# Scores of two heads side by side in float32 from head 18 on, and a mixing addition at high priority

## The chip, the cores and the metric

The kernel runs on one core of a Trainium2 chip. A core has TensorE (PE; PEld is its loading of weights) for matmuls, VectorE (DVE) and ScalarE (ACT) for work on elements, GpSimd (POOL) for the same beside them, and SyncE (SP), which issues the DMAs here. Each engine takes its instructions in order and waits at semaphores for the others. The metric is the time of one execution on the device in microseconds, the median of several runs.

## The reference

Attention over blocks of 64 tokens, a mixing of tokens and channels, and a gate, in float32. There are 8 sequences of 8 heads, 576 tokens and 64 elements a head; the channels are 512.

```
scores = scale * q @ k.T                    # 64 heads of 576 x 576, depth 64
scores = where(block_i >= block_j, scores, -1e9)
attn = softmax(scores);  x = attn @ v       # heads side by side: 8 x 576 x 512
h = (x.T @ U) @ V;  u = x + h.T             # mixing of tokens, rank 32
x = u + max(u @ w_ch1, 0) @ w_ch2           # mixing of channels, 2048 wide
gate = sigmoid(causal convolution of x, 5 taps)
out = (gate * (x @ w_val)) @ w_out
```

## The kernel before

The heads are walked in order. The kernel writes the order of TensorE's instructions itself; those of the other engines are put in order by a scheduler, from the order of the program and from priorities. A generator `attention` steps through the heads in ticks. The tick of head n computes its scores, its maximum and its exponentials, and, two heads behind, the products of the weights with v (`emit_pv`). Between them stand the steps of the mixing of tokens for the pairs before: T (transposes), G (product with U) and H (product with V, then the addition to x).

After the heads of the first sequence the channel mixing runs too, over nine groups of 512 tokens. Each of its steps s is a block of twelve matmuls of 512 columns into h (`emit_h1`, L841) and twelve into acc (`emit_o`, L887). In the midst of each block and behind it, `gap` takes steps of the generator, as a pace set by counts allows. So a tick is spread over several blocks, and a `yield` in it is a place where a block of six matmuls can stand.

Most matmuls are done in float32r: an operand is split into a high part, which float32r keeps, and the rest as a second float32r number, and three matmuls add the products. A matmul in float32 itself shows as two records of weights and matmul in the trace, one in float32r as one.

The 64 heads have two forms. Heads 0 to 17 (`n < NQ`) compute scores with rows and columns exchanged (`emit_q_bank`), in float32. From head 18 on, which the change is about, before has `prep_qk` and `emit_s_piece`:

- `prep_t` transposes q and k of a pair of heads on VectorE into `tq` and `tk`. Head a of the pair owns rows 64a to 64a + 63.
- `prep_qk` makes of them for one head operands of 128 rows: `qs` has the high part of q on the head's own rows and the rest on the other 64, `ks` the high part of k on both halves, and `kl` the rest of k on its own rows and zeros on the others. This takes three casts on ScalarE (L93) and a memset (L380) and two subtractions (L99) on GpSimd.
- `emit_s_piece` makes the scores of one head in four groups, with a yield behind each. The groups have query columns of 64, 192 and 256 (one PSUM buffer), 320, 448 and 320. Each piece takes two matmuls, `ks` with `qs` (L397) and `kl` with `qs` (L398). ScalarE copies the group to SBUF (L402).

PSUM buffers for scores (pS), products with v (pPV) and the mixing steps (pT, pG, pH) come from one ring of four (L204, `ABUF`). The SBUF tiles for scores, `s0` and `s1`, have two buffers each. Behind the scores come memsets at the masked corners on GpSimd (`emit_corners`), the maximum over keys on VectorE (`emit_max_a`, `_b`, `_c`), the subtraction (L528) and the exponentials (L550).

The keys of heads 0 to 17 lie padded with zeros in four tiles, whose room `ks` and `qs` take over. `mix_H` adds the product with V to x (L713) and by that also frees the PSUM buffer pH; x goes on to `u`, the operand of the channel mixing. `behind(0)` in it does nothing, since no instruction is noted under 0.

Of the kernel before, what the change touches and what calls it, by code (L numbers as in the profile page):

```python
# [8 lines left out]
F32 = mybir.dt.float32  # L9
F32R = mybir.dt.float32r  # L10
# [7 lines left out]
P = 128  # L18
# [4 lines left out]
def attn_moe_gate_kernel(ctx: ExitStack, tc: tile.TileContext, q, k, v, U, V, w1, w2, wval, convw, wout, out):  # L23
    nc = tc.nc
    B, H, S, D = q.shape
# [8 lines left out]
    NP = H // 2  # L34
# [21 lines left out]
    ABUF = 4  # L56
    RAWB = 2
    WAB = 2
    QV = 10
    KV = 0  # L60
    UVE = 0
    HPOS = 8
    GPOS = 6
# [1 line left out]
    PRE = 2  # L65
    CV0 = 1
    CV1 = 3
    MX0 = 0
    TP0 = 0
    NR0 = 0  # L70
    MM0 = 0
# [3 lines left out]
    NQ = FIRST_SPLIT  # L75
# [11 lines left out]
    def f32(ap):  # L87
        return ap if ap.dtype == F32 else ap.bitcast(F32)

    vec, act, pool, pe, sp = nc.vector, nc.scalar, nc.gpsimd, nc.tensor, nc.sync  # L90

    def hi_act(o, i):
        act.copy(o, i)  # L93
# [4 lines left out]
    def lo(eng, o, i, h):  # L98
        eng.tensor_tensor(o, i, f32(h), op=ALU.subtract)  # L99
# [13 lines left out]
    def behind(at):  # L113

        return tc.issue_after(mark[at]) if at in mark else nullcontext()
# [83 lines left out]
    st_p = rpool("stp", 1)  # L199
    s_p = rpool("sp", 2)  # L200
# [85 lines left out]
    sw = []  # L286
# [17 lines left out]
    def setup_att():  # L304
        for t in vstk:
            pool.memset(t[:, :, D:P], 1.0)
            pool.memset(t[0:D, NK - 1, :], 0.0)
        for a in range(2):
            for t in kz:
                pool.memset(t[a][own[1 - a]], 0.0)  # L310

    raw = {}

# [23 lines left out]
    stk = {}  # L337

    own = [slice(0, D), slice(D, P)]
    def pads(nm, dtype):  # L340
        return [st_p.tile([P, S], dtype, tag=f"{nm}{a}", name=f"{nm}{a}") for a in range(2)]

    kz = [pads(nm, F32) for nm in ("ks", "qs")]
    ks, qs = [], []
    kl = st_p.tile([P, S], F32R, name="kl")
    qkt = {}

    def prep_t(pn):
        if pn >= B * NP:
            return  # L350
        t = raw.pop(pn)
        if 2 * pn < NQ:
            tq = rot("tk" if pn % 2 else "tq", 1)
            z = kz[pn % 2]
            for rows in own if pn == 0 else (slice(0, P),):
                vec.transpose(tq[rows], t["q"][rows])
                for a in range(2):
                    if pn or rows == own[a]:
                        vec.transpose(z[a][own[a]], t["k"][own[a]])
            qkt[pn] = (tq, z)  # L360
        else:
            tq, tk = rot("tq", 1), rot("tk", 1)
            vec.transpose(tq, t["q"])
            vec.transpose(tk, t["k"])
            qkt[pn] = (tq, tk)
        load_qk(pn + 1)

    def prep_qk(n):
        if n >= B * H or n < NQ:
            return  # L370
        if not ks:
            ks.extend(pads("ks", F32R))
            qs.extend(pads("qs", F32R))
        tq, tk = qkt[n // 2]
        a = n % 2
        me, ot = own[a], own[1 - a]
        hi_act(qs[a][me], tq[me])
        hi_act(ks[a][me], tk[me])
        hi_act(ks[a][ot], tk[me])
        pool.memset(f32(kl[ot]), 0.0)  # L380
        lo(vec if n < KV else pool, kl[me], tk[me], ks[a][me])
        lo(vec if n < QV else pool, qs[a][ot], tq[me], qs[a][me])

    def kslice(j):
        return slice(q0[j], q0[j] + P) if q0[j] + P <= S else slice(S - P, S)

    stt = {}

    def emit_s_piece(n, i):
        pr, a = divmod(n, 2)  # L390
        if i == 0:
            stt[n] = [s_p.tile([P, w], F32, tag=f"s{h}", name=f"s{h}") for h, w in enumerate(sw)]
        ps = psum["a"].tile([P, 512], F32, tag="a", name="pS")
        o = 0
        for j, a0, a1 in pieces[i]:
            w = a1 - a0
            pe.matmul(ps[:, o:o + w], ks[a][:, kslice(j)], qs[a][:, a0:a1], start=True, stop=False)  # L397
            pe.matmul(ps[:, o:o + w], kl[:, kslice(j)], qs[a][:, a0:a1], start=False, stop=True)  # L398
            o += w
        j, a0, a1 = pieces[i][0]  # L400
        d = soff[j] + a0 - q0[j]
        act.copy(stt[n][half_of[j]][:, d:d + o], ps[:, 0:o])  # L402


    qbanks = [
# [14 lines left out]
    def emit_q_bank(n, i):  # L420

        a = n % 2
        tq, z = qkt[n // 2]
        if i == 0:
            s0, s1 = (s_p.tile([P, w], F32, tag=f"s{h}", name=f"s{h}") for h, w in enumerate(sw))
            eqs[n] = {3: s0[:, 0:4 * P], 1: s0[:, 4 * P:6 * P], 0: s1[:, 0:P], 2: s1[:, P:4 * P], 4: rot("m" if a else "mb", 1)}
            t = tiny_p.tile([P, 2 * NTT + 2], F32, tag="rq", name="rq")
            qmax[n] = (t[:, 0:NTT + 1], t[:, NTT + 1:], psum["a"].tile([P, 512], F32, tag="a", name="pS"))
        r, nm, _ = qmax[n]
        ps = psum["a"].tile([P, 512], F32, tag="a", name="pS") if i else _  # L430
        for t, k0, k1, o in qbanks[i]:
            pe.matmul(ps[:, o:o + k1 - k0], tq[:, kslice(t)], z[a][:, k0:k1], start=True, stop=True)
        if i == 0:
            vec.memset(ps[0:D, 4 * P - D:4 * P], MASKED)
        elif i == 2:
            vec.memset(ps[0:D, 3 * P - D:3 * P], MASKED)
        elif i == 3:
            vec.memset(ps.rearrange("p (c w) -> p c w", w=D)[0:D, 1:6:4, :], MASKED)
        for t, k0, k1, o in qbanks[i]:
            c = t + (k0 > 0)  # L440
            vec.reduce_max(r[:, c:c + 1], ps[:, o:o + k1 - k0], axis=AX.X)
        if i == 0:
            x = vec.tensor_scalar(nm[:, 3:4], r[:, 3:4], -scale, None, op0=ALU.mult)
        elif i == 2:
            vec.tensor_tensor(r[:, 4:5], r[:, 4:5], r[:, 5:6], op=ALU.max)
            x = vec.tensor_scalar(nm[:, 2:5:2], r[:, 2:5:2], -scale, None, op0=ALU.mult)
        elif i == 3:
            x = vec.tensor_scalar(nm[:, 0:2], r[:, 0:2], -scale, None, op0=ALU.mult)
        if i == 1:
            eqs[n]["wait"] = ps  # L450
            return
        noted(1, x)
        noted(3, x)
        for t, k0, k1, o in qbanks[i] + (qbanks[1] if i == 2 else []):
            src = eqs[n]["wait"] if i == 2 and t == NTT - 1 and k0 == 0 else ps
            act.activation(eqs[n][t][:, k0:k1], src[:, o:o + k1 - k0], AF.Exp, bias=nm[:, t:t + 1], scale=scale)
# [241 lines left out]
    def mix_H(pn, i):  # L698
        pcs = mix_pieces(pn // NP)
        if i >= len(pcs):  # L700
            return
        gi, a0, a1, off = pcs[i]
        if gi >= 2 and gi > y_done[0] + 2:
            later.append((pn, i))
            return
        xt = xts[pn]
        d = pn % NP
        uh, ul = u_tiles(gi)
        w = a1 - a0
        ps = ps_p.tile([P, 512], F32, tag="a", name="pH")  # L710
        pe.matmul(ps[:, 0:w], gst[pn], vst[:, a0:a1], start=True, stop=True)
        with behind(MX0 if pn < NP else 0):
            vec.tensor_tensor(xt[:, a0:a1], ps[:, 0:w], xt[:, a0:a1], op=ALU.add)  # L713
        hi_act(uh[:, d, off:off + w], xt[:, a0:a1])
        lo(pool, ul[:, d, off:off + w], xt[:, a0:a1], uh[:, d, off:off + w])
# [7 lines left out]
    def tick(n, mixed, last=B * NP):  # L723


        e = n - DEPTH
        new, old = n < NH, 0 <= e < NH

        load_v(e + 1)
        for i in range(4):  # L730
            if n < NQ:
                emit_q_bank(n, i)
            elif new:
                emit_s_piece(n, i)
            if i == 3 and new and n >= NQ:
                emit_corners(n)
                emit_max_a(n)
            yield
        if new:
            if n >= NQ:  # L740
                emit_max_b(n)
            if n % 2 == 1:
                prep_t((n + 1) // 2)
            prep_qk(n + 1)
        yield from mixing(2 * e, mixed, last)
        if new and n >= NQ:
            for _ in emit_max_c(n):
                pass
            emit_sub(n, 0)
            emit_sub(n, 1)  # L750
        if old:
            emit_pv(e, 0)
            yield
        if new and n >= NQ:
            emit_exp(n)
        if old:
            emit_pv(e, 1)
        prep_v(e + 1)
        emit_est(e + 1)
        if old:  # L760
            if e % 2 == 1:
                with tc.high_priority() if URG and e == H - 1 else ExitStack():
                    emit_norm_a(e // 2)
                    emit_norm_b(e // 2)
            yield
        yield from mixing(2 * e + 1, mixed, last)
# [247 lines left out]
        split_w2(f)  # L1014
    setup_att()
    prep_t(0)
    prep_qk(0)
    pb1 = ExitStack()
    pbp = {}

# [151 lines left out]
```

## Time and profile before

| what | value |
|---|---|
| time, median of 3 runs | 1533.32 us (1531.53 to 1535.98) |
| the profiled execution | 1538.09 us, its span 1536.3 us |
| PE busy | 1427.0 us, 93% of the span, 6664 instructions |
| DVE busy | 1146.3 us, 75% |
| ACT busy | 789.5 us, 51% |
| POOL busy | 516.1 us, 34% |
| granted TensorE clock, mean | 0.976 |

Busy is the time in which an engine has an instruction in flight. Matmuls overlap: one of 512 columns has a record of about 0.40 us, and the next one starts 0.23 us after it. A clock of 1 is 2.4 GHz, and 0.5 is 1.2 GHz. The time has a little more than the span, which goes from the first instruction to the last. The idle time of an engine is put down to the instruction whose end released it.

### The profile page before, as it was taken

Reading aid. Unit: us, or ns where it says so; the run is one execution under the profiler, and the core shown is the slowest. Engines: PE = TensorE matmul, PEld = TensorE weight load, DVE = VectorE, ACT = ScalarE, POOL = GpSimd, SP = SyncE. Lnnn points to the kernel's source line nnn. Section 1 sums busy time; section 2 is a strip of 40 time slices with the busy share of each in tenths; the row PEclk is TensorE's granted clock in tenths of the full one; section 3 lists DMA queues with packets and bytes.
Section 4 is the critical chain, followed back from the end, with each engine's and each line's share of the span. In section 5 each row is a group of like instructions: output and inputs, shape, how many; then the busy total and the mean of one; then the engine's idle time right before and its main releaser. Section 6 shows DMA issues by size and latency. Waiting matters only on the chain. (4 is left out here: it accounts for less than half of the span.)

```text
span 1536.3 us, 20391 instructions
## 1 busy us (share of the span) xinstructions
PE 1427.0 (93%) x6664; PEld 1151.1 (75%) x6664; DVE 1146.3 (75%) x2252; ACT 789.5 (51%) x1639; POOL 516.1 (34%) x587
## 2 busy tenths in 40 slices
PE   5897899979989998999899989989999999999999
PEld 2665677868767787777687778768888888778887
DVE  7887874659887888788888878887624427399991
ACT  4785565546565665666476556655512212243432
POOL 3133232333435333534443444335104210353410
PEclk8998999989999999999999999999999999999999
DMA  7555662224233333333323333232225543323221
GB/s 171 142 133 167 204 194 79 79 80 103 79 81 114 85 86 105 92 79 89 109 79 90 92 92 93 78 85 90 77 83 198 174 135 123 105 68 103 78 74 69
DMA packets 246291, 163.58 MB, mean 106 GB/s; under 512 B 197669, under 2 KB 212261, under 8 KB 246186
## 3 DMA queue, kind: packets, MB, share of 16 engines
q1 hardware_dynamic: 246186, 162.29, 36.6%
q8 instruction: 53, 0.87, 0.2%
q14 instruction: 52, 0.43, 0.1%
HBM read 134.98 MB, written 27.26 MB: 106 GB/s over the span
## 5 line engine op out<-in xcount | busy, mean ns | idle before, releaser
L887 PE MATMUL acc<-hh,w 128*128 128x512 f32 x1152 | 408.4, 405 | 10.2 <-ACT hh L869 10.2
L887 PEld LDWEIGHTS acc<-hh,w 128*128 128x128 f32 x1152 | 220.7, 192 | 57.7 <-ACT hh L869 12.8
L841 PE MATMUL h<-uh,w1hi 128*128 128x512 f32 x576 | 239.1, 415 | 9.9 <-DVE hl L870 6.3
L887 PE MATMUL acc<-hl,w 128*128 128x512 f32 x576 | 230.2, 400 | 5.9 <-DVE hl L870 5.9
L841 PE MATMUL h<-uh,w1lo 128*128 128x512 f32 x576 | 228.2, 396 | 0.0
L841 PE MATMUL h<-ul,w1hi 128*128 128x512 f32 x576 | 228.0, 396 | 0.0
L870 DVE SCALAR_TENSOR_TENSOR hl<-h,hh 128x512 fp32r<-128x512 f32 x144 | 98.2, 682 | 116.1 <-ACT hh L869 115.4
L869 ACT ACTIVATE hh<-h 128x512 fp32r<-128x512 f32 x144 | 85.8, 596 | 154.3 <-PE h L841 147.4
L550 ACT ACTIVATE s<-s 128x448 f32<-128x448 f32 x92 | 65.5, 712 | 150.0 <-DVE s L528 149.0
L841 PEld LDWEIGHTS h<-uh,w1hi 128*128 128x128 f32 x576 | 110.7, 192 | 35.8 <-DVE hl L870 8.2
L402 ACT COPY s<-pS 128x320 f32<-128x320 f32 (+2 forms) x184 | 89.8, 490 | 80.9 <-PE pS L398 77.2
L887 PEld LDWEIGHTS acc<-hl,w 128*128 128x128 f32 x576 | 110.5, 192 | 27.5 <-DVE hl L870 8.2
L841 PEld LDWEIGHTS h<-uh,w1lo 128*128 128x128 f32 x576 | 109.7, 190 | 24.8
L841 PEld LDWEIGHTS h<-ul,w1hi 128*128 128x128 f32 x576 | 110.7, 192 | 18.3 <-issue 1.4
L528 DVE TENSOR_TENSOR s<-s,mb 128x64 f32<-128x64 f32 (+4 forms) x230 | 123.0, 598 | 1.3
L962 DVE SCALAR_TENSOR_TENSOR gt<-yb,cw,gt 128x516 f32<-128x516 f32 (+1 forms) x144 | 116.5, 839 | 1.4
L99 POOL TENSOR_TENSOR vlo<-vstk,vhi 128x320 fp32r<-128x320 f32 x46 | 54.3, 1180 | 161.1 <-ACT vhi L93 148.1
L99 POOL TENSOR_TENSOR yl<-yb,yh 128x512 fp32r<-128x512 f32 (+7 forms) x64 | 67.7, 1091 | 96.9 <-ACT yh L93 96.8
L99 POOL TENSOR_TENSOR ul<-xt,uh 128x512 fp32r<-128x512 f32 (+7 forms) x64 | 53.2, 840 | 132.6 <-ACT uh L93 131.9
L397 PE MATMUL pS<-qs,ks 128*128 128x320 f32 (+4 forms) x276 | 80.4, 309 | 6.3 <-ACT lt L614 4.2
L398 PE MATMUL pS<-qs,kl 128*128 128x320 f32 (+4 forms) x276 | 82.4, 302 | 0.0
L99 DVE TENSOR_TENSOR el<-s,eh 128x448 fp32r<-128x448 f32 x92 | 76.7, 859 | 5.2 <-issue 4.6
(152 smaller groups left out, 3105.5 us busy)
## 6 DMA issues: line engine op xcount, KB each, us to landing
w<-w_s SPq DMA_DIRECT2D x144, 512.0 KB, 3.2
rawq<-in_q_dram SPq DMA_DIRECT2D x128, 72.0 KB, 2.4
rawk<-in_k_dram SPq DMA_DIRECT2D x128, 72.0 KB, 2.5
out_dram<-ot SPq DMA_DIRECT2D x35, 256.0 KB, 2.0
raw<-in_moe_w_ch_dram SPq DMA_DIRECT2D x64, 128.0 KB, 2.3
raw<-in_moe_w_ch_dram SPq DMA_DIRECT2D x16, 512.0 KB, 4.2
vstk<-in_v_dram SPq DMA_DIRECT2D x64, 128.0 KB, 2.6
w_s<-wo SPq DMA_DIRECT2D x16, 512.0 KB, 3.6
```

Of the source, the lines that this page charges most:

```text
L99: eng.tensor_tensor(o, i, f32(h), op=ALU.subtract)
L397: pe.matmul(ps[:, o:o + w], ks[a][:, kslice(j)], qs[a][:, a0:a1], start=True, stop=False)
L398: pe.matmul(ps[:, o:o + w], kl[:, kslice(j)], qs[a][:, a0:a1], start=False, stop=True)
L402: act.copy(stt[n][half_of[j]][:, d:d + o], ps[:, 0:o])
L528: noted(3, vec.tensor_tensor(sv(n, j), sv(n, j), mb[:, q0[j]:], op=ALU.subtract))
L550: act.activation(s, s, AF.Exp, scale=scale)
L841: pe.matmul(ps[:, 0:n], w[:, d, fs], x[:, d, 0:n], start=(d == 0 and i == 0), stop=(d == ND - 1 and i == 2))
L869: act.activation(hh[:, 0:n], ps[:, 0:n], AF.Relu)
L870: latest[0] = vec.scalar_tensor_tensor(hl[:, 0:n], ps[:, 0:n], 0.0, f32(hh[:, 0:n]), op0=ALU.max, op1=ALU.subtract)
L887: pe.matmul(acc[d][:, 0:n], w[:, wi, ds], x[:, 0:n], start=(f == 0 and i == 0), stop=(f == NF - 1 and i == 2))
L962: vec.scalar_tensor_tensor(gt[d][:, 0:gw], y[:, d, j:j + gw], cw[:, d, j:j + 1], gt[d][:, 0:gw], op0=ALU.mult, op1=ALU.add)
```

## The change

For pairs 9 to 31 (heads 18 to 63) `prep_qk` and all its operands are gone. `emit_s_piece` now works on a pair, in the tick of its even head: for each piece one float32 matmul for either head, straight from `tk` and `tq`, with rows 0 to 63 for the even head and 64 to 127 for the odd one, into a PSUM buffer for each. In the odd tick the four yields stay, without scores. The corners and the first part of the maximum come behind the fourth group for the even head as before, and for the odd head at the first step of its own tick.

As the scores of two heads are now made at once, a third pair of score tiles is needed: heads with n % 3 == 1 take the tiles `za` and `zb`, which held the padded keys of the first heads, now as one tile for both heads of a pair. The addition in `mix_H` is traced at high priority, so the scheduler puts it ahead of other work that is ready.

```diff
-    QV = 10
-    KV = 0
...
-    MX0 = 0
...
-                pool.memset(t[a][own[1 - a]], 0.0)
+                pool.memset(t[own[1 - a], a, :], 0.0)
...
-    def pads(nm, dtype):
-        return [st_p.tile([P, S], dtype, tag=f"{nm}{a}", name=f"{nm}{a}") for a in range(2)]
-
-    kz = [pads(nm, F32) for nm in ("ks", "qs")]
-    ks, qs = [], []
-    kl = st_p.tile([P, S], F32R, name="kl")
+    def spare(nm, n):
+        return st_p.tile([P, n], F32, tag=nm, name=nm)
+
+    kz = [spare(nm, 2 * S).rearrange("p (a s) -> p a s", s=S) for nm in ("za", "zb")]
...
-    def prep_qk(n):
...
-        tq, tk = qkt[n // 2]
-        a = n % 2
-        me, ot = own[a], own[1 - a]
-        hi_act(qs[a][me], tq[me])
-        hi_act(ks[a][me], tk[me])
-        hi_act(ks[a][ot], tk[me])
-        pool.memset(f32(kl[ot]), 0.0)
-        lo(vec if n < KV else pool, kl[me], tk[me], ks[a][me])
-        lo(vec if n < QV else pool, qs[a][ot], tq[me], qs[a][me])
-
...
-    def emit_s_piece(n, i):
-        pr, a = divmod(n, 2)
+    def emit_s_piece(pn, i):
+
+        heads = (2 * pn, 2 * pn + 1)
+        tq, tk = qkt[pn]
         if i == 0:
-            stt[n] = [s_p.tile([P, w], F32, tag=f"s{h}", name=f"s{h}") for h, w in enumerate(sw)]
-        ps = psum["a"].tile([P, 512], F32, tag="a", name="pS")
+            for n in heads:
+                stt[n] = [spare(("za", "zb")[h], w) if n % 3 == 1 else s_p.tile([P, w], F32, tag=f"s{h}", name=f"s{h}") for h, w in enumerate(sw)]
+        ps = [psum["a"].tile([P, 512], F32, tag="a", name="pS") for _ in own]
         o = 0
         for j, a0, a1 in pieces[i]:
             w = a1 - a0
-            pe.matmul(ps[:, o:o + w], ks[a][:, kslice(j)], qs[a][:, a0:a1], start=True, stop=False)
-            pe.matmul(ps[:, o:o + w], kl[:, kslice(j)], qs[a][:, a0:a1], start=False, stop=True)
+            for t, me in zip(ps, own):
+                pe.matmul(t[:, o:o + w], tk[me, kslice(j)], tq[me, a0:a1], start=True, stop=True)
             o += w
         j, a0, a1 = pieces[i][0]
         d = soff[j] + a0 - q0[j]
-        act.copy(stt[n][half_of[j]][:, d:d + o], ps[:, 0:o])
+        for n, t in zip(heads, ps):
+            act.copy(stt[n][half_of[j]][:, d:d + o], t[:, 0:o])
...
-        with behind(MX0 if pn < NP else 0):
+        with tc.high_priority():
             vec.tensor_tensor(xt[:, a0:a1], ps[:, 0:w], xt[:, a0:a1], op=ALU.add)
...
-            elif new:
-                emit_s_piece(n, i)
-            if i == 3 and new and n >= NQ:
+            elif new and n % 2 == 0:
+                emit_s_piece(n // 2, i)
+            if i == (0 if n % 2 else 3) and new and n >= NQ:
                 emit_corners(n)
                 emit_max_a(n)
...
-            prep_qk(n + 1)
```

In the changed kernel lines move up by 17 to 19: the score matmul is L380, its copy L385, the addition of the mixing L696, hh and hl L851 and L852.

On TensorE, the first group of scores of a head before, between two blocks of h (names are output<-moving operand, weights; the shape is that of the weights' columns and the moving columns):

```order
L841 MATMUL h_2682<-uh,w1lo 128x512
L841 MATMUL h_2682<-uh,w1hi 128x512
L841 MATMUL h_2682<-ul,w1hi 128x512
L841 MATMUL h_2682<-uh,w1lo 128x512
L397 MATMUL pS<-qs_2603,ks_2601 128x64
L398 MATMUL pS<-qs_2603,kl 128x64
L397 MATMUL pS<-qs_2603,ks_2601 128x192
L398 MATMUL pS<-qs_2603,kl 128x192
L397 MATMUL pS<-qs_2603,ks_2601 128x256
L398 MATMUL pS<-qs_2603,kl 128x256
L841 MATMUL h_2682<-uh,w1hi 128x512
```

The same place now; x2 are the matmuls of the two heads:

```order
L823 MATMUL h_2669<-uh,w1lo 128x512
L823 MATMUL h_2669<-uh,w1hi 128x512
L823 MATMUL h_2669<-ul,w1hi 128x512
L823 MATMUL h_2669<-uh,w1lo 128x512
L380 MATMUL pS<-tq,tk 128x64 x2
L380 MATMUL pS<-tq,tk 128x192 x2
L380 MATMUL pS<-tq,tk 128x256 x2
L823 MATMUL h_2669<-uh,w1hi 128x512
```

Six matmuls of 128 rows for one head have become six of 64 rows for two heads; the blocks around them are the same, and at the odd head's tick nothing stands between them.

On ScalarE, one head's copies of scores (L402) before, among the exponentials of the head before (L550) and the casts (L93) of q and k for the next one:

```order
L93 CAST x<-pT 64x128
L402 COPY s_5083<-pS 128x512
L550 ACTIVATE s_4906<-s_4906 128x448
L869 ACTIVATE hh<-h_5074 128x512
L402 COPY s_5083<-pS 128x320
L550 ACTIVATE s_4907<-s_4907 128x768
L402 COPY s_5084<-pS 128x448
L93 CAST ks_2602<-tk 64x576 x2
L402 COPY s_5084<-pS 128x320
L93 CAST qs_2604<-tq 64x576
```

Now, in the tick of an even head (s_ and za, zb are the score tiles of its two heads):

```order
L851 ACTIVATE hh<-h_6713 128x512
L385 COPY s_6769<-pS 128x512
L385 COPY za<-pS 128x512
L385 COPY s_6769<-pS 128x320
L385 COPY za<-pS 128x320
L385 COPY s_6770<-pS 128x448
L385 COPY zb<-pS 128x448
L385 COPY s_6770<-pS 128x320
L385 COPY zb<-pS 128x320
L851 ACTIVATE hh<-h_6809 128x512
L90 CAST uh<-xt 128x256
```

The casts are gone, and the eight copies of a pair stand together between two relus of h.

On VectorE, the addition of the mixing before (L713), the transpose of the next k, and the maximum of one head (m, t, r):

```order
L713 TENSOR_TENSOR xt<-pH,xt 128x320
L364 STREAM_TRANSPOSE tk<-rawk 128x576
L870 SCALAR_TENSOR_TENSOR hl<-h_5636,hh 128x512
L490 TENSOR_TENSOR m<-s_5604,s_5605 128x448
L492 TENSOR_TENSOR m<-m,s_5605 128x320
L492 TENSOR_TENSOR m<-m,s_5604 128x192
L492 TENSOR_TENSOR m<-m,s_5604 128x64
L500 STREAM_TRANSPOSE t<-m 128x448
L502 TENSOR_REDUCE r_5668<-t 128x18
L99 TENSOR_TENSOR el<-s_5432,eh 128x448
L99 TENSOR_TENSOR el<-s_5433,eh 128x768
```

Now (L696 is the addition, L852 the rest of h; za and zb hold the scores of one head, s_ those of the other):

```order
L358 STREAM_TRANSPOSE tq<-rawq 128x576
L359 STREAM_TRANSPOSE tk<-rawk 128x576
L473 TENSOR_TENSOR m<-za,zb 128x448
L696 TENSOR_TENSOR xt<-pH,xt 128x320
L852 SCALAR_TENSOR_TENSOR hl<-h_5439,hh 128x512
L475 TENSOR_TENSOR m<-m,zb 128x320
L475 TENSOR_TENSOR m<-m,za 128x192
L475 TENSOR_TENSOR m<-m,za 128x64
L483 STREAM_TRANSPOSE t<-m 128x448
L485 TENSOR_REDUCE r_5473<-t 128x18
L473 TENSOR_TENSOR m<-s_5401,s_5402 128x448
```

The addition now stands right behind the first step of a maximum, the transposes of q and k stand ahead of it together, and the maxima of the pair's two heads run into each other.

## Rows read from the trace of the kernel before

**Rows 1.** Stage of heads 18 to 63: start:end, length, busy us of each engine (instructions), PEclk, DMA.

```profile
262.00:1100.00 838.00, 778.70 (x3784) 644.30 (x3783) 696.66 (x1362) 497.73 (x1015) 338.96 (x413) 0.97 0.33 90
```

**Rows 2.** Groups of TensorE, 262 to 1100 us: busy, mean ns | idle before, releasers.

```profile
L887 PE MATMUL acc<-hh,w 128*128 128x512 f32 x744 | 267.5, 406 | 10.2 <-ACT hh L869 10.2
...
L841 PE MATMUL h<-uh,w1hi 128*128 128x512 f32 x373 | 154.5, 414 | 6.7 <-DVE hl L870 3.2 <-ACT lt L614 2.3 <-ACT s L402 0.6
...
L887 PE MATMUL acc<-hl,w 128*128 128x512 f32 x372 | 149.8, 403 | 5.9 <-DVE hl L870 5.9
...
L397 PE MATMUL pS<-qs,ks 128*128 128x320 f32 (+4 forms) x276 | 80.4, 309 | 6.3 <-ACT lt L614 4.2 <-DVE x L99 1.9
...
L612 PE MATMUL pPV<-eh,vhi 128*128 128x448 f32 x132 | 49.4, 374 | 11.5 <-DVE hl L870 11.5
...
L672 PE MATMUL pT<-ident,xt 128*128 128x128 f32 x92 | 14.3, 279 | 6.4 <-DVE xt L713 6.4
...
L680 PE MATMUL pT<-ident,xt 128*64 128x128 f32 x23 | 6.5, 284 | 8.4 <-DVE xt L713 8.4
```

**Rows 3.** TensorE's timeline around the scores of one head: start, length in us.

```profile
588.57 0.19 PE L397 MATMUL pS<-qs,ks 128*128 128x64 f32 x1
...
588.71 0.34 PE L397 MATMUL pS<-qs,ks 128*128 128x192 f32 x1
...
589.25 0.39 PE L841 MATMUL h<-uh,w1hi 128*128 128x512 f32 x1
...
590.64 0.31 PE L397 MATMUL pS<-qs,ks 128*128 128x320 f32 x1
...
590.94 0.39 PE L887 MATMUL acc<-hh,w 128*128 128x512 f32 x1
...
592.32 0.37 PE L397 MATMUL pS<-qs,ks 128*128 128x448 f32 x1
...
592.73 0.40 PE L887 MATMUL acc<-hh,w 128*128 128x512 f32 x1
...
594.10 0.31 PE L397 MATMUL pS<-qs,ks 128*128 128x320 f32 x1
...
594.40 0.39 PE L841 MATMUL h<-uh,w1hi 128*128 128x512 f32 x1
```

**Rows 4.** TensorE's timeline around two float32 matmuls of an earlier head.

```profile
229.78 1.88 PE L432 MATMUL pS<-ks,tq 128*128 128x512 f32 x4
...
231.73 0.40 PE L841 MATMUL h<-ul,w1hi 128*128 128x512 f32 x1
231.96 0.40 PE L841 MATMUL h<-uh,w1lo 128*128 128x512 f32 x1
```

**Rows 5.** Groups of ScalarE, 262 to 1100 us.

```profile
L402 ACT COPY s<-pS 128x320 f32<-128x320 f32 (+2 forms) x184 | 89.8, 490 | 80.9 <-PE pS L398 77.2 <-DVE r L518 1.9 <-DVE el L99 1.4
...
L93 ACT CAST ks<-tk 64x576 fp32r<-64x576 f32 x88 | 59.0, 671 | 8.4 <-PE pS L397 6.0 <-DVE tk L364 1.4
...
L93 ACT CAST qs<-tq 64x576 fp32r<-64x576 f32 x44 | 29.5, 671 | 0.5
```

**Rows 6.** Groups of GpSimd, 262 to 1100 us.

```profile
L99 POOL TENSOR_TENSOR qs<-tq,qs 64x576 fp32r<-64x576 f32 x45 | 69.0, 1533 | 8.3 <-ACT qs L93 5.7
...
L99 POOL TENSOR_TENSOR kl<-tk,ks 64x576 fp32r<-64x576 f32 x45 | 64.4, 1431 | 3.1
...
L380 POOL MEMSET kl<- 64x576 f32 x45 | 25.9, 575 | 74.4 <-PE pS L398 65.8 <-DVE hl L870 4.0 <-DVE t L499 4.0
```

**Rows 7.** The copy of 32x18 (min/median/max in the second row), and one collision.

```profile
L516 DVE COPY r<-r 32x18 f32<-32x18 f32 x46 | 41.2, 896 | 1.5
...
L516 DVE COPY r<-r x46: 166/168/1904, 285.3 to 1093.6; 32x18 f32<-32x18 f32 x46
...
738.63 1.41 POOL L99 TENSOR_TENSOR kl<-tk,ks 64x576 fp32r<-64x576 f32 x1
...
739.33 0.88 DVE L518 COPY r<-r 64x18 f32<-64x18 f32 x1
```

More of the change, by code (lines that the diff above doesn't have):

```diff
@@ L358, in prep_t @@
                     if pn or rows == own[a]:
-                        vec.transpose(z[a][own[a]], t["k"][own[a]])
+                        vec.transpose(z[own[a], a, :], t["k"][own[a]])
             qkt[pn] = (tq, z)
@@ L366, in prep_t @@
         load_qk(pn + 1)
-    def prep_qk(n):
[L369 to L373, printed above, removed]
-        tq, tk = qkt[n // 2]
-        a = n % 2
-        me, ot = own[a], own[1 - a]
-        hi_act(qs[a][me], tq[me])
-        hi_act(ks[a][me], tk[me])
-        hi_act(ks[a][ot], tk[me])
-        pool.memset(f32(kl[ot]), 0.0)
-        lo(vec if n < KV else pool, kl[me], tk[me], ks[a][me])
-        lo(vec if n < QV else pool, qs[a][ot], tq[me], qs[a][me])
     def kslice(j):
@@ L431, in emit_q_bank @@
         for t, k0, k1, o in qbanks[i]:
-            pe.matmul(ps[:, o:o + k1 - k0], tq[:, kslice(t)], z[a][:, k0:k1], start=True, stop=True)
+            pe.matmul(ps[:, o:o + k1 - k0], tq[:, kslice(t)], z[:, a, k0:k1], start=True, stop=True)
         if i == 0:
@@ L1016, in attn_moe_gate_kernel @@
     prep_t(0)
-    prep_qk(0)
     pb1 = ExitStack()
```

## The prediction

> **What bounds the kernel now.** I read three views in this order: the busy time by stage, then the idle time of TensorE inside the stage that changes, then single stretches of its timeline. The scores of heads 18 to 63 run from about 262 to 1100 us, woven between the blocks of the channel mixer (h, acc). In these 838 us TensorE has a record in flight for 778.7, VectorE for 696.7, ScalarE for 497.7 and GpSimd for 339.0 [rows 1]. So TensorE is nearly full, and a change can move the time in two ways only: by the array time of the scores, or by the 59.3 us in which TensorE stands idle, to which comes the granted clock of 0.97 there, worth at most 838 x 0.03 = 25 us (the clock has the levels 1.2 and 2.4 GHz, and 0.97 is their mix). Of the 59.3 us, seven groups hold 55.4, and each was released by VectorE or ScalarE: by hl 11.5 + 5.9 us, by hh 10.2, by the mixing addition xt (L713) 6.4 + 8.4, and 6.7 before h and 6.3 before pS behind hl and behind copies that empty PSUM [rows 2]. No wait of the scores for data stands among them. These are delays of two loaded queues, VectorE at 83% and ScalarE at 59%, and not one long chain.
>
> **The scores on TensorE.** Before, one head takes 12 float32r matmuls in four groups. From the start of a group to the start of the matmul behind it: 588.57 to 589.25 (0.68 us), 590.64 to 590.94 (0.30), 592.32 to 592.73 (0.41), 594.10 to 594.40 (0.30) [rows 3]. That is 1.69 us a head and 3.38 a pair; 23 pairs make 78 us.
>
> After, a pair has 12 float32 matmuls on 64 rows each, six for either head. The price of a float32 matmul is in the first heads' scores: two of 512 columns, four records, begin at 229.78. The block behind them has its second matmul at 231.73, and one of its matmuls takes 231.96 - 231.73 = 0.23, so the scores ended at about 231.50 [rows 4]: 0.43 us a record, two records a matmul, 0.84 ns a column and pass. By that a pass is 0.27 us at 320 columns, 0.38 at 448, 0.22 at 256, 0.16 at 192; at 64 I take 0.07, since two records of 64 fit between 588.57 and 588.71 [rows 3]. No row of before has a matmul on 64 rows, so how far the two heads overlap is bounded from both sides. Not at all: four passes after each other, 4 x (0.07 + 0.16 + 0.22 + 0.27 + 0.38 + 0.27) = 5.48 us a pair, +2.1, and 23 pairs make +48. Fully: two passes, 2.74 us, -0.64, in all -15. I take what lies between. In the queue stand A's first pass, A's second, B's first, B's second. A's second pass needs the same rows as A's first; B's first can run beside A's second; B's second then runs alone. A group that stands alone costs three passes: 0.81 + 1.14 + 0.81 for the single pieces. Within the first group of three pieces the halves interlock, about 0.07 + 0.07 + 0.16 + 0.16 + 0.22 + 0.22 + 0.22 = 1.12. That is 3.88 a pair, +0.50, and **+12 us** over 23 pairs. In the order of the changed kernel nearly every group does stand alone between two blocks: 90 groups for 23 x 4.
>
> At each of these groups the array goes from 128 rows to 64 and back. Rows of before show matmuls of one kind following each other 0.23 us apart while each has 0.40 us from start to end [rows 4]: 0.17 us of every matmul lie under the next one. If a change of rows let nothing overlap, 2 x 90 changes would cost up to 180 x 0.17 = 31 us; the lower end is nothing, since a change can't make the matmul before it shorter. I take nothing, the nearest row being the 128x128 transposes, float32r and float32 matmuls that already follow each other here without a gap of their own, and keep 31 for the rivals.
> By the Trainium skill, "TensorEngine Tiling (Array Packing)", Key Properties, changing the tiling mode, not just the tile, drains the engine. No row here shows such a change of mode, so the trace neither agrees nor differs; by that rule the sum would be 31 us worse than mine, and it is a rival below.
>
> **What goes from the other engines.** ScalarE loses two casts of k and one of q a head: 59.0 + 29.5 = 88.5 us of the stage's 497.7 [rows 5]. GpSimd loses two subtractions and a memset: 69.0 + 64.4 + 25.9 = 159 of 339 [rows 6]. VectorE loses no instruction, but time: a copy of 32x18 has a median of 168 ns and a mean of 896 [rows 7], so 46 x 0.73 = 33 us of it are spent standing still. The copy of 64x18 at 739.33 took 0.88 us while kl's subtraction ran on GpSimd from 738.63 to 740.04 [rows 7]. Not all such delays are due to the subtractions that go; xt's scaling and y's addition stay. By the share of GpSimd's time that goes I count about half, some 20 to 30 us of 697.
>
> None of that is on TensorE's queue, so it counts only as far as the waits of [rows 2] shrink. The addition of the mixing at high priority aims at 6.4 + 8.4 = 14.8 us; it also waits in VectorE's queue for its matmul pH, so I take 10 and not all. Of the other 40.6 us I take 12: VectorE's load falls from 83% to about 80%, ScalarE's from 59 to 49%, and waits behind a queue fall faster than its load. With 22 of 59.3 us of idle time gone, the same share of the 25 us of clock, 9, comes back. Together **-31 us**; the bounds are 0 and the 55.4 us of the named waits with their part of the clock, 79. What hides: nothing queued on GpSimd or ScalarE becomes late by the removal; next in line are the same waits for hl and hh.
>
> **What is added elsewhere.** The eight copies of scores (0.49 us each, [rows 5]) of a pair now stand together in the even head's tick, in ScalarE's queue ahead of hh and the exponentials, and none in the odd one; their number stays 184. The transposes of q and k now feed the matmuls directly, from single buffers, but the score matmuls that read them stand half a pair's work ahead of the next transposes, so I count nothing. The third pair of score tiles takes the place of the padded keys; est of the head three before has read it by then. Both maximum chains of a pair fall together on VectorE; that is within the bounds of the relief.
>
> **Sum.** The profiled execution had 1538.1 us (span 1536.3, the rest lies around it); 1538.1 + 12 - 31 = 1519. The median of the runs is 4.8 lower, 1533.3, so on that scale **1514 us**.
>
> **The rivals.**
> Full overlap: the two heads' first passes also start together, -15 instead of +12. For it: a group's operands lie on separate rows, in separate PSUM tiles. Against: each matmul is two records in the queue, and the queue has shown only one matmul after the other. 1533.3 - 15 - 31 = 1487 us.
> By the Trainium skill, "TensorE: Matmul & The Clock Gate", Part 3, matmuls on different row groups start about 4 ns apart and run together; no run here shows it, and by that the sum would be nearest to this case.
> No side by side at all: the float32 matmuls of 64 rows run one after the other, and the change does not do what its words say. The place is the four groups of a pair, the price +48; it decides from the point at which less than a third of the passes overlap, since the relief is 31. For it: all matmuls in the trace of before follow one another. 1533.3 + 48 - 31 = 1550 us, slower.
> Changing the rows costs: overlap as forecast, but each change of rows exposes up to 0.17 us, +31. For it: the tail under the next matmul is there in [rows 4]. Against: no present change of kind exposes it. 1533.3 + 12 + 31 - 31 = 1545 us, slower.
> PSUM in the place of casts: a group takes two of the four PSUM buffers that scores, PV, transposes, G and H share, and the next group waits for two copies. If every second of the 90 groups waits for one copy more, 45 x 0.49 = 22 us. For it: pS already waits 6.3 us for buffers [rows 2], and the copies stand together. Against: a block of six matmuls, about 1.4 us, stands between groups, and two copies take 1.0. 1533.3 + 12 + 22 - 31 = 1536 us, no change.
>
> **How the numbers follow.** Forecast 0.47, full overlap 0.12, no overlap 0.17, changes of rows 0.13, PSUM 0.11. The forecast's own range is 1500 to 1527 (relief of 18 to 45 us). What a measurement can tell from no change is 0.3%, 4.6 us, so 1528.7 to 1537.9 is the same. Faster: 0.47 + 0.12 = 0.59. Same: the PSUM case, 0.11. Slower: 0.17 + 0.13 = 0.30. The range from 1487 to 1556 takes in the centres of all cases; outside are a relief near zero with no overlap, and more relief than 31 with full overlap, together about 0.15 to 0.2.
>
> **What would show it.** On TensorE a pair's group of 320 columns should span about 0.8 us to the next block: 1.1 would be no overlap, 0.55 full, 1.0 and more with a late start of the next block the changes of rows. ScalarE's busy time should fall by about 90 us, GpSimd's by about 160, the 32x18 copy's mean below 600 ns. The waits for xt should be near 5 us and TensorE's idle time between 262 and 1100 us near 37. If the idle time is not below 50, the relief is wrong; if the groups stand at 1.1 us, the overlap is, and the kernel is slower.

## The result and the profile after

| | before | after |
|---|---|---|
| median of the runs, us | 1532.98 (1531.53 to 1535.98) | 1518.50 (1518.03 to 1519.19) |
| profiled execution, us | 1538.09, span 1536.3 | 1519.19, span 1517.4 |
| granted clock over the span | 0.976 | 0.974 |

The kernel became faster by 1.0%: ratio 0.9903, 95% interval 0.9886 to 0.9921. The forecast was 1514. The sum came out within 5 us; its terms did not.

The stage of heads 18 to 63 again, in the columns of [rows 1]:

```profile
262.00:1100.00 838.00, 801.06 (x3881) 616.00 (x3881) 640.29 (x1369) 423.93 (x900) 176.94 (x280) 0.97 0.35 92
```

TensorE is busy 801 instead of 779 us, so 36.9 us are idle instead of 59.3. ScalarE is down 74, GpSimd 162, VectorE 56 us. The mean clock is the same, 0.97. (The window now holds a little more of the program, since everything comes sooner: the last score matmul begins at 1051.2 instead of 1085.3 us.)

What TensorE waits for there (engine, line, releaser: us in total, times, longest):

```profile
PE pT L663 <- DVE xt L696: 28.8, 5, 5.9
PE pT L655 <- DVE xt L696: 7.9, 1, 7.9
PE pS L380 <- ACT s L385: 0.2, 1, 0.2
```

Compare [rows 2]: the waits for hl, hh, lt and copies, 40.6 us, are gone but for 0.2. The waits for the mixing addition xt, the only ones the high priority aims at, grew from 14.8 to 36.7.

One score group of 320 columns on TensorE's timeline (start, length), the counterpart of the groups in [rows 3]:

```profile
581.58 0.39 PE L823 MATMUL h<-uh,w1lo 128*128 128x512 f32 x1
581.90 0.81 PE L380 MATMUL pS<-tq,tk 64*128 64x320 f32 x4
582.64 0.50 PE L869 MATMUL acc<-hh,w 128*128 128x512 f32 x1
582.98 0.39 PE L869 MATMUL acc<-hl,w 128*128 128x512 f32 x1
```

The starts of the group's four records in the trace are 581.901, 581.908, 582.274 and 582.281. So the two heads' records start 7 ns apart and run side by side, and the group takes two passes, 0.37 us each by their starts, though one pass of 320 columns should take 0.27 by [rows 4]. Before the group stands a gap: the last block matmul begins at 581.58 and the first score at 581.90, 0.32 us instead of 0.23. Behind it the first block matmul takes 0.50 instead of 0.39, and the next begins 0.34 after it instead of 0.23.

So that entry and exit are counted, I take a group's room from the last block matmul before it to the second behind it, less two matmuls of 0.23: 582.98 - 581.58 - 0.46 = 0.94 us. The medians over all groups are 1.38 (three pieces), 0.94 twice (320) and 1.16 (448): 4.42 us a pair. The same reckoning gives 0.69, 0.30, 0.42 and 0.30 a head before, 3.41 a pair. The scores cost 1.0 us more a pair, **+23 us** over 23 pairs.

Two of the small copies on VectorE, for [rows 7] (busy, mean ns | idle before):

```profile
L499 DVE COPY r<-r 32x18 f32<-32x18 f32 x46 | 9.3, 201 | 1.5
L491 DVE COPY r<-r 64x18 f32<-64x18 f32 x46 | 7.9, 172 | 1.4
```

The casts of k and q, the subtractions and the memset of [rows 5, 6] are gone. The copy of 32x18 whose mean was 896 ns (L516) is L499 now, with a mean of 201: VectorE hardly stands still there any more.

One of the five long waits, on VectorE's and TensorE's timelines:

```profile
879.67 0.33 PE L694 MATMUL pH<-vst,g 128*128 128x384 f32 x1
...
887.46 0.42 PE L663 MATMUL pT<-ident,xt 128*64 128x128 f32 x1 [5.62 <-DVE xt L696]
...
888.53 0.63 PE L823 MATMUL h<-uh,w1lo 128*128 128x512 f32 x1
888.96 0.63 PE L823 MATMUL h<-uh,w1hi 128*128 128x512 f32 x1
```

```profile
880.36 0.67 DVE L881 TENSOR_TENSOR y<-acc,uh 128x512 f32<-128x512 f32 x1
880.96 1.14 DVE L511 TENSOR_TENSOR za<-za,mb 128x64 f32<-128x64 f32 x3
...
883.07 1.13 DVE L495 COPY r<-r 32x18 f32<-32x18 f32 x1
884.23 2.11 DVE L96 TENSOR_TENSOR el<-s,eh 128x448 fp32r<-128x448 f32 x2
886.26 0.68 DVE L881 TENSOR_TENSOR y<-acc,uh 128x512 f32<-128x512 f32 x1
886.86 0.54 DVE L696 TENSOR_TENSOR xt<-pH,xt 128x384 f32<-128x384 f32 x1
```

The product pH was ready soon after 879.67. Its addition begins at 886.86, behind 6.5 us of older work in VectorE's queue. Then the clock is at its lower level: matmuls 0.43 us apart at 888.53 and 888.96 instead of 0.23, until about 893.

Without the high priority the changed code gives the same program, with the same order of instructions on every engine: that edit does nothing. The addition's new place on VectorE, right behind the first step of a maximum, comes from the other edits.

### The profile page after: what moved, and what is told of

The parts are those of the page before. It is cut to its first block, busy times and chain, and to the rows that moved or that the text cites. A ratio compares the mean times of both kernels' runs of the same rounds, so it can differ in the third digit from the quotient of the medians.

```text
span 1517.4 us, 20100 instructions
## 1 busy us (share of the span) xinstructions
PE 1431.7 (94%) x6664; PEld 1108.1 (73%) x6664; DVE 1084.2 (71%) x2252; ACT 705.5 (46%) x1501; POOL 348.9 (23%) x449
## 4 chain that ended last, share of the span: by engine, by line
PE 78%; DVE 14%; DMA 3%; issue 2%; ACT 2%; SPq 1%; POOL 0%; DVEq 0%; ACTq 0%; POOLq 0%
PE acc L869 24%; PE h L823 24%; PE pPV L595 8%; PE o L986 7%; PE pS L380 6%; PE val L962 5%; PE pS L415 2%; DMA raw<-in_moe_w_ch_dram 1%; PE pG L671 1%; DVE rq L424 1%; DVE s L511 1%; DVE y L881 1%; DVE m L475 1%; DVE wa L124 1%; PE pT L655 1%
## 5 line engine op out<-in xcount | busy, mean ns | idle before, releaser
L823 PE MATMUL h<-uh,w1hi 128*128 128x512 f32 x576 | 242.9, 422 | 3.1 <-DVE hl L852 3.1
L852 DVE SCALAR_TENSOR_TENSOR hl<-h,hh 128x512 fp32r<-128x512 f32 x144 | 98.5, 684 | 133.0 <-ACT hh L851 131.7
L851 ACT ACTIVATE hh<-h 128x512 fp32r<-128x512 f32 x144 | 86.0, 597 | 200.6 <-PE h L823 194.6
L96 POOL TENSOR_TENSOR vlo<-vstk,vhi 128x320 fp32r<-128x320 f32 x46 | 42.9, 932 | 372.9 <-ACT vhi L90 354.1
L380 PE MATMUL pS<-tq,tk 64*128 64x320 f32 (+4 forms) x552 | 91.8, 429 | 0.2 <-ACT s L385 0.2
L596 ACT COPY xt<-pPV 64x128 f32<-64x128 f32 (+1 forms) x128 | 50.1, 392 | 75.5 <-PE pPV L595 73.7
L385 ACT COPY s<-pS 128x512 f32<-128x512 f32 (+2 forms) x124 | 58.2, 496 | 50.4 <-PE pS L380 49.1
L533 ACT ACTIVATE s<-s 128x448 f32<-128x448 f32 (+1 forms) x62 | 44.0, 710 | 73.1 <-DVE s L511 73.1
L511 DVE TENSOR_TENSOR s<-s,mb 128x64 f32<-128x64 f32 (+4 forms) x155 | 71.4, 524 | 0.3
L882 POOL TENSOR_TENSOR y<-y,ul 128x512 f32<-128x512 f32 x32 | 46.8, 1469 | 90.8 <-DVE y L881 86.4
```

The costliest lines, as they stand in the source:

```text
L380: pe.matmul(t[:, o:o + w], tk[me, kslice(j)], tq[me, a0:a1], start=True, stop=True)
L385: act.copy(stt[n][half_of[j]][:, d:d + o], t[:, 0:o])
L511: noted(3, vec.tensor_tensor(sv(n, j), sv(n, j), mb[:, q0[j]:], op=ALU.subtract))
L823: pe.matmul(ps[:, 0:n], w[:, d, fs], x[:, d, 0:n], start=(d == 0 and i == 0), stop=(d == ND - 1 and i == 2))
L851: act.activation(hh[:, 0:n], ps[:, 0:n], AF.Relu)
L852: latest[0] = vec.scalar_tensor_tensor(hl[:, 0:n], ps[:, 0:n], 0.0, f32(hh[:, 0:n]), op0=ALU.max, op1=ALU.subtract)
```

## Experiments

Theory A at the start: the two heads overlap fully, and what they gain is lost on the changes between 128 and 64 rows; and the relief came through GpSimd and VectorE. What makes the long waits was open: the two maximum chains of a pair were tried first, then the rest of VectorE's queue. The rivals stand in each expectation.

**Do the heads overlap?** Both heads on the first head's rows:

```
-            for t, me in zip(ps, own):
+            for t, me in zip(ps, (own[0], own[0])):
```

> The changed kernel, with the second head's score matmuls on the first head's 64 rows (its scores are those of the first head; everything else as it was). Nothing can overlap on the same rows. Theory A (full overlap before): a pair's scores go from two passes to four, +2.74 us, 63 us in all, about 1580 us. Theory B (three passes before): +1.6 us a pair, 37 us, about 1555. If there was no overlap: 1518, no change.

Measured 1578.84 us, 60 more than the changed kernel; ratio to the kernel before 1.0294 (1.0262 to 1.0325). Its group of 320 columns:

```profile
605.41 0.39 PE L823 MATMUL h<-uh,w1lo 128*128 128x512 f32 x1
605.73 1.34 PE L380 MATMUL pS<-tq,tk 64*128 64x320 f32 x4
607.00 0.50 PE L869 MATMUL acc<-hh,w 128*128 128x512 f32 x1
607.34 0.40 PE L869 MATMUL acc<-hl,w 128*128 128x512 f32 x1
```

Its room is 607.34 - 605.41 - 0.46 = 1.47 instead of 0.94. The overlap is real, and worth 60 us against no overlap. The gaps at entry (0.32) and exit (0.50, 0.34) stay as they were, so they don't come from the overlap.

**What do the changes of rows cost?** The same without overlap, but over all 128 rows, so that no change is left:

```
-                pe.matmul(t[:, o:o + w], tk[me, kslice(j)], tq[me, a0:a1], ...)
+                pe.matmul(t[:, o:o + w], tk[:, kslice(j)], tq[:, a0:a1], ...)
```

> Both heads' score matmuls of the changed kernel over all 128 rows (each then computes the sum of the two heads' scores, so the scores are left out as such). No matmul of a group can then overlap the other head's, and no change between 128 and 64 rows is left. Its counterpart is the kernel in which both heads used the first head's 64 rows (1578.84 us; no overlap either, but with the changes; its groups stood 2.357, 1.466 and 1.909 us apart). Theory A: a change to 64 rows and back costs some 0.41 us a group: groups of about 1.95, 1.06 and 1.50 us, 90 groups, 37 us less: 1535-1548 us. Rival B: the changes are free and the extra time belongs to float32 matmuls as such: the same group times as there, 1574-1584 us.

Measured 1543.71 us (1.0076, 1.0049 to 1.0103), 35.1 less than with 64 rows:

```profile
593.22 0.40 PE L823 MATMUL h<-uh,w1lo 128*128 128x512 f32 x1
593.45 1.24 PE L380 MATMUL pS<-tq,tk 128*128 128x320 f32 x4
594.29 0.63 PE L869 MATMUL acc<-hh,w 128*128 128x512 f32 x1
594.76 0.40 PE L869 MATMUL acc<-hl,w 128*128 128x512 f32 x1
```

The first score begins 0.23 after the block matmul, as any matmul does, and the room is 594.76 - 593.22 - 0.46 = 1.08. The medians are 1.97, 1.08 and 1.51 against 2.36, 1.47 and 1.91: 0.39 us a group, and 90 groups make 35.1 us, which is the measured difference. (The two ran on different chips, where the kernel before took 1534.65 and 1531.74 us; by the ratios the difference is 33 us.) Theory A holds: one change to 64 rows and back costs 0.39 us.
By the Trainium skill, "TensorEngine Tiling (Array Packing)", Key Properties, changing the tiling mode drains TensorE. The trace agrees, and puts a price to it: 0.39 us a round trip.

These groups also price the passes without changes: 1.97 + 2 x 1.08 + 1.51 = 5.64 us a pair with no overlap, so 2.82 with full overlap, 0.59 less than before.

**Fewer changes.** Groups 1 and 2, 3 and 4 of a pair back to back, so half the changes:

```
-            elif new and n % 2 == 0:
+            elif new and n % 2 == 0 and i % 2 == 0:
                 emit_s_piece(n // 2, i)
+                emit_s_piece(n // 2, i + 1)
```

> The changed kernel, with the four groups of scores of a pair issued as two: the first and second back to back, the third and fourth back to back. Half the changes between 64 and 128 rows go. Theory A (the two heads overlap fully, and each change of rows costs about 0.2 us): 92 changes fewer, 18 us less, about 1500 us, if the four PSUM buffers don't make TensorE wait. Theory B, the prediction's (three passes a group, changes of rows free): two joined groups interlock and save a pass, about 0.4 us a pair, 9 us less, about 1509. Theory C (the PSUM ring decides): the second of two joined groups waits for copies, and the time is 1518 or more.

Measured 1502.04 us (0.9785, 0.9762 to 0.9809): the fastest kernel of all, but only in small part by the mechanism. TensorE's blocks and, from a second view, the queue around one joined group:

```profile
576.97 0.39 PE L824 MATMUL h<-uh,w1lo 128*128 128x512 f32 x1
577.28 2.72 PE L380 MATMUL pS<-tq,tk 64*128 64x64 f32 x16
...
580.27 0.39 PE L824 MATMUL h<-ul,w1hi 128*128 128x512 f32 x1
```

```profile
578.57 0.59 ACT L385 COPY s<-pS 128x512 f32<-128x512 f32 x1 [0.41 <-PE pS L380]
579.20 0.29 PEld L380 LDWEIGHTS pS<-tq,tk 64*128 64x128 f32 x2 [0.65 <-ACT s L385]
```

The joined group's room is 580.27 - 576.97 - 0.46 = 2.84 us, while the two single groups take 1.38 + 0.94 = 2.32. The second head's 320 columns wait for a PSUM buffer until the copy of 578.57 has emptied it, and the overlap is lost there. Not every joined group waits. Groups 3 and 4 of another pair:

```profile
446.78 0.39 PE L870 MATMUL acc<-hh,w 128*128 128x512 f32 x1
447.10 1.56 PE L380 MATMUL pS<-tq,tk 64*128 64x448 f32 x8
...
448.93 0.40 PE L870 MATMUL acc<-hl,w 128*128 128x512 f32 x1
```

Their room is 448.93 - 446.78 - 0.46 = 1.69 us, where the two single groups take 1.16 + 0.94 = 2.10: 0.41 less, about the price of one visit. Over all 46 joined groups the two cases mix: with their waits a pair takes 4.9 us on average, against 4.5 in the changed kernel, 9 us more over 23 pairs. So the gain lies in the stage's other rows:

```profile
262.00:1100.00 838.00, 809.90 (x3967) 635.32 (x3966) 621.90 (x1379) 426.19 (x907) 177.85 (x282) 1.00 0.36 93
```

```profile
PE pT L663 <- DVE xt L696: 8.4, 5, 1.8
...
PE pT L655 <- DVE xt L696: 4.9, 1, 4.9
```

The waits for xt are 13.3 instead of 36.7 us, and the granted clock is 1.00 instead of 0.97. Theory A's number was hit, but its saving shows only where no buffer is waited for, and the wait that C named takes more than that back. What made the kernel faster is that the long waits are gone, and with them the lower clock. Why this order avoids them was not taken apart.

**Are two maximum chains in a heap the cause of the long waits?** The odd head's chain put back to the end of its tick:

```
-            if i == (0 if n % 2 else 3) and new and n >= NQ:
+            if i == 3 and new and n >= NQ:
```

> The changed kernel, with the odd head's corners and the start of its maximum back at the fourth step of its own tick. Theory A (the six waits of some 6 us for the mixing addition, 36.7 us in all, come from the two maximum chains of a pair falling together on VectorE): these waits fall below 15 us, and the time by 15 to 25 us, to about 1498. Rival (VectorE's queue at a sequence's end is late whatever the tick does): waits of 30 us or more and 1515 to 1520 us.

Measured 1515.38 us (0.9890, 0.9869 to 0.9910), and the waits for xt are 28.8 + 7.9 us, the same to a tenth. The chains are not the cause.

**Where did the relief come from?** GpSimd's work put back, read by nobody:

```
+        pool.memset(f32(kl[ot]), 0.0)
+        lo(pool, kl[me], tk[me], tq[me])
+        lo(pool, kl[ot], tq[me], tk[me])
```

> The changed kernel, with the memset and the two subtractions of 64x576 a head back on GpSimd, into a tile that nobody reads. Theory A (much of the relief came through VectorE, which stood still behind GpSimd's subtractions): 15 to 25 us slower, about 1537, and the copy of 32x18 back at a mean of some 800 ns. Rival (the relief came from ScalarE's casts): within 5 us of 1518.

Measured 1575.93 us (1.0272, 1.0247 to 1.0297), 57 more than the changed kernel, and more than was expected. Waits for hl are back (before pPV too, 6.4 us, and for lt 4.9), and those for xt are longer still:

```profile
PE pT L677 <- DVE xt L710: 35.6, 5, 7.8
PE pT L669 <- DVE xt L710: 7.2, 1, 7.2
PE acc L884 <- DVE hl L867: 6.5, 11, 1.3
```

```profile
L505 DVE COPY r<-r 64x18 f32<-64x18 f32 x44 | 25.9, 588 | 1.4
```

GpSimd has room for it (347 of 838 us in the stage), TensorE waits for none of its results, and VectorE for 30 us of them in all, against 34 in the changed kernel. What suffers is VectorE: its instructions last longer. The copy that [rows 7] show at a mean of 896 ns stays short (210), so the sign that A named did not come; but other instructions of the same chain grew. The copy of 64x18 above had a mean of 172 (L491). In the 25 cases in which no two-operand work runs on GpSimd beside it, it takes 170 to 174 ns; in the 19 in which some does, 1290 in the median. VectorE is busy 672 instead of 640 us in the stage, with two heads fewer done there, and what waits for VectorE waits longer. TensorE's idle time in the stage is 68.9 us.

The same for ScalarE's three casts:

```
+        hi_act(kl[me], tq[me])
+        hi_act(kl[me], tk[me])
+        hi_act(kl[ot], tk[me])
```

> The changed kernel with three 64x576 copies of qs/ks a head put back on ScalarE (into an unread tile), as the kernel before had three casts there. Theory A: the waits that vanished on TensorE (40.6 us to 0.2) went through GpSimd's and VectorE's work, ScalarE's casts had room. Then ScalarE's busy time in 262-1100 us is some 75 us above the changed kernel's 424 us, TensorE's idle time there stays within 37-42 us, and the time is 1518-1526 us. Rival B: ScalarE's casts held up exponentials and hh as much as GpSimd held up the rest: half of the 57 us that GpSimd's work cost, 1540-1550 us, with waits for hh above 5 us.

```profile
262.00:1100.00 838.00, 802.86 (x3893) 618.64 (x3892) 633.03 (x1374) 511.90 (x1034) 176.65 (x281) 0.98 0.35 91
```

Measured 1515.21 us (0.9882, 0.9854 to 0.9910): 88 us more on ScalarE cost nothing. So the relief came by way of GpSimd, and of what its work does to VectorE.

**What makes the long waits?** The five subtractions queued behind the addition (an order given to VectorE's queue, no new wait):

```
+            for n, i, kind in held:
+                if n == top and kind == 0:
+                    tc.add_manual_dep(i, x.ins.name, ...)
```

> The changed kernel with the five subtractions of the maximum (za/zb) of the current step queued on VectorE behind the deferred addition of the mixing. Theory A: the five waits of 5.6-5.9 us for xt come from VectorE's queue, in which y, five subtractions, r and el stand ahead of the addition; 2.1 us of them less each is 11 us, and the lower clock after each wait goes partly with them: xt waits 15-27 us instead of 36.7, the time 1490-1508 us. Rival B: y and el stay ahead and end last all the same, or the exponentials, which now start later, hold TensorE for as long: xt waits fall but waits for e take their place, 1515-1525 us.

Measured 1516.17 us (0.9886, 0.9853 to 0.9919).

```profile
PE pH L700 <- DVE hl L866: 13.7, 4, 3.9
PE h L837 <- ACT lt L603: 8.0, 5, 1.8
PE pT L669 <- DVE xt L702: 6.4, 5, 2.3
PE pT L661 <- DVE xt L702: 6.1, 1, 6.1
```

The waits for xt fell to 12.5 us, as A had it, but TensorE now waited for hl and lt instead, 22.2 us that the changed kernel does not have. The time is rival B's, and so is the change of names, though B had named the exponentials and not hl. With the joined groups beside it:

> Both edits together: groups 1 and 2, 3 and 4 of a pair back to back (1502.04 us alone) and the five subtractions behind the deferred addition of the mixing. Theory A: what is left of the waits for xt there, 13.3 us, falls to 5-9 us; since the clock is 0.986 there already, little comes beside it: 1493-1500 us. Rival B: the joined groups already took what the order on VectorE can give: 1500-1506 us.

Measured 1523.02 us (0.9936, 0.9913 to 0.9959), 21 slower than the joined groups alone, outside of both ranges:

```profile
PE pH L700 <- DVE hl L867: 22.2, 5, 4.9
```

The order that frees xt costs hl more than it saves.

**Is it the PSUM buffer that TensorE waits for?** At the long waits ScalarE empties PSUM and GpSimd adds:

```
-            vec.tensor_tensor(xt[:, a0:a1], ps[:, 0:w], xt[:, a0:a1], op=ALU.add)
+            act.copy(t, ps[:, 0:w])
+            pool.tensor_tensor(xt[:, a0:a1], t, xt[:, a0:a1], op=ALU.add)
```

> The changed kernel in which a deferred addition of the mixing (some 20 pieces, one at each of the five long waits) leaves VectorE: ScalarE copies the product out of PSUM and GpSimd adds it to xt. Theory A: TensorE waits at those places for the PSUM buffer that the addition gives back; it stood 5 us behind y, five subtractions, r and el in VectorE's queue, and ScalarE, with half its time free, gives it back within 1.5 us. Waits for xt fall from 36.7 us to 8-16, and the lower clock behind each goes too: 1485-1505 us. Rival B: as when the subtractions were put behind it (1516.17), another step of VectorE's queue at the same place (hl, y, the subtractions of x) holds TensorE in its stead: waits change names, 1510-1522 us.

```profile
PE pT L663 <- ACT kl L699: 13.2, 5, 3.1
PE pH L694 <- DVE hl L864: 8.0, 5, 3.3
PE pT L655 <- ACT kl L699: 4.0, 1, 4.0
```

```profile
880.03 0.30 PE L663 MATMUL pT<-ident,xt 128*64 128x128 f32 x1 [3.09 <-ACT kl L699]
...
881.07 1.72 POOL L700 TENSOR_TENSOR xt<-kl,xt 128x384 f32<-128x384 f32 x1
```

Measured 1512.51 us (0.9861, 0.9829 to 0.9893). The transposes pT now wait for ScalarE's copy, which only empties the buffer and writes nothing that they read; the addition behind it is GpSimd's, and begins after the transpose. So it is the buffer that they wait for. The wait is shorter, 17.2 us in all, but over half of what it lost (8.0 and 3.2 us of 19.5) stands behind hl instead: the mechanism is A's, the time B's. With the joined groups:

> The same edit with groups 1 and 2, 3 and 4 of a pair issued back to back (1502.04 us alone). Theory A: the joined order had already moved the long waits away (13.3 us of xt left), so the edit gives 0-8 us: 1494-1503 us. Rival B: the joined order was lucky in where its sequences end, any shift of VectorE's queue brings such waits back (as the subtractions behind the addition did, 1523.02 us): 1508-1525 us.

```profile
PE h L836 <- ACT lt L597: 11.2, 5, 2.9
```

Measured 1516.97 us (0.9890, 0.9866 to 0.9915). The waits for xt's buffer are at 2.1 us, others stand in their place, and the kernel is still 15 slower than the joined groups alone. B's range holds, but not its words: such waits as before did not come back. That the 1502 us depend on where VectorE's queue happens to stand at a sequence's end is what these two runs speak for; they don't show it. Nothing that was tried on top of that order kept its time.

## Why the prediction came out right

**TensorE is the bound, and only array time and idle time count.** Right. ScalarE's 88 us were worth nothing (1515.21 with them put back); every change of the time showed on TensorE.

**Scores, +12: two steps failed, in opposite directions.** "A group that stands alone costs three passes" was wrong: the two heads' records start 7 ns apart, full overlap, two passes. By the room of groups without a change of rows that is 2.82 us a pair against 3.41 before, 0.59 x 23 = -14 us; the rival had -15.
By the Trainium skill, "TensorE: Matmul & The Clock Gate", Part 3, matmuls on different row groups start about 4 ns apart; the trace agrees in kind, with 7.
"I take nothing" for the changes of rows was wrong too: 0.39 to 0.40 us a group, 90 groups, +35 to +37 us; the bound from the 0.17 us that a matmul lies under the next, 31 us, was a little short. Together that is the +23 of the profile, 11 more than forecast. The two rivals both came true, and each took back part of the other; by luck their sum is nearer to the forecast than either alone. The prediction's sign could not tell them from it: from its start to the next block the group of 320 columns spans 582.64 - 581.90 = 0.74 us, which reads as the 0.8 of three passes. It took the gaps at entry and exit and the starts of the records to see two passes and the changes.

**Relief, -31: 42, and wrong in its parts.** The profiled executions differ by 18.9 us with +23 in the scores, so 42 came back elsewhere, 11 more than forecast. This miss and that of the scores cancel: on the scale of the profiled executions the sum said 1519, and 1519.19 was measured, by luck. (The medians stand 4.5 apart because the profiled execution of before lay 5.1 us above its median and that of the changed kernel only 0.7.) Of the 42, 22.4 are TensorE's idle time in the stage (59.3 to 36.9; "near 37" was foreseen, but from parts that both failed, as below). Another 8 are, by an estimate, the tails of waits: an idle stretch begins at the end of a record, 0.17 us after the next matmul could have started [rows 4], and there are 47 fewer waits (54 before, 7 after). Some 7 are the clock's. About 5 us are not assigned; some of them are groups of before that ran longer than the median I set against them.
- "I take 10" of xt's 14.8 us: failed, the waits grew by 21.9. The priority moves nothing. The addition stands behind work that is ready and older, and TensorE waits for the PSUM buffer behind it.
- "Of the other 40.6 us I take 12": mis-sized, 40.4 went. The prediction counted 20 to 30 us off VectorE, from one copy; its busy time in the stage fell by 56. GpSimd's two-operand work had slowed more of VectorE's instructions than that copy; put back, it costs 57.
- "9 us of clock come back": about 7 did, though the mean clock stayed at 0.97. The sums over the stage's stretches at the lower level, eleven before and six after:

```profile
sum 44.40, PE 42.45 PEld 34.88 DVE 37.16 ACT 19.38 POOL 16.02; mean PE 3.86 PEld 3.17 DVE 3.38 ACT 1.76 POOL 1.46
...
sum 44.40, PE 28.60 PEld 22.98 DVE 42.10 ACT 17.04 POOL 21.88; mean PE 4.77 PEld 3.83 DVE 7.02 ACT 2.84 POOL 3.65
```

They last as long as before, but now TensorE stands idle in a third of them and works in 28.6 instead of 42.5 us. At half speed that is 14 us lost instead of 21, by an estimate. What is left lies behind the six long waits, one stretch at each; the joined groups, without five of them, had 1.00.

**PSUM in the place of casts.** It did not come: pS waits 0.2 us. It came at once when groups were joined.

**Range and rivals.** The four cases were set apart as if only one could hold. Full overlap and the changes are independent, and their joint case, 1533.3 - 14 + 36 - 31 = 1524, had no line.

## What to carry to other kernels

Two matmuls on separate halves of the rows do run side by side, but each visit to such a group from matmuls over all rows costs 0.39 us here, as much as a whole pass of 448 columns (0.38 by [rows 4]); count the visits before the overlap, and make them few and long, with a PSUM buffer for every tile of them. Work that is free on its own engine can still be dear: the subtractions on GpSimd slowed VectorE's instructions, and what waits for VectorE paid. A mean clock over a stage counts idle time too: look in which stretches the engine was working when it fell. When a wait's releaser is an addition late in a queue, ask which buffer it gives back, and what will stand last in that queue once it is moved.

## What the runs showed that I had not expected

- Where the 0.4 us of a visit lie, in the group at 581.90: 0.09 ahead of it (0.32 instead of 0.23), 0.11 behind the first block matmul (0.34 instead of 0.23), and 0.20 between (581.90 to 582.64 for two passes of 0.27). Over 128 rows float32 matmuls enter without a gap (593.22, 593.45). The loading of weights, in the changed kernel and over 128 rows, shows a part of it:

```profile
581.90 0.30 PEld L380 LDWEIGHTS pS<-tq,tk 64*128 64x128 f32 x4 [0.36 <-ACT s L385]
582.64 0.19 PEld L869 LDWEIGHTS acc<-hh,w 128*128 128x128 f32 x1 [0.44 <-issue]
...
593.22 0.96 PEld L380 LDWEIGHTS pS<-tq,tk 128*128 128x128 f32 x4
```

Over 128 rows the first score's weights load from 593.22 on, under the block matmul and 0.23 us ahead of their own. At a visit the load begins only with its matmul, at 581.90, and again on the way back, at 582.64. The copy named as the releaser is not the reason: the entry takes 0.32 us at each of the 90 groups.
- 57 us for 170 us of unread GpSimd work (346.79 - 176.94 in the stage), on an engine that is idle for more than half of the stage.
- Each of the six waits of TensorE, 5.6 to 7.9 us long, is followed by 3.0 to 6.1 us of its work at the lower clock level.
